# Pooled attention and channel mix: due dates, load order, engines of the first chunks' small steps, and the generator's clock changed

## The chip, the cores and the metric

One Trainium2 (trn2) chip, one NeuronCore of it. The metric is the device time of the whole program in microseconds (us), the median of several executions. The engines are named as in the profile: PE (TensorE), DVE (VectorE), ACT (ScalarE), POOL (GpSimd) and SP, whose queue issues every DMA of this kernel.

## What is computed

```python
def _attn_ref(q, k, v):                      # q, k, v: (8, 8, 576, 64), float32
    k_p = k.reshape(B, H, 72, 8, D).mean(axis=3)      # keys and values pooled by 8
    v_p = v.reshape(B, H, 72, 8, D).mean(axis=3)
    scores = scale * np.matmul(q, k_p.transpose(0, 1, 3, 2))
    scores = scores - np.max(scores, axis=-1, keepdims=True)
    attn = np.exp(scores)
    attn = attn / (np.sum(attn, axis=-1, keepdims=True) + 1e-09)
    return np.matmul(attn, v_p)

def _moe_ref(x, mu_k, mu_r, w_k, w_v, w_r):  # x: (8, 576, 512), the heads side by side
    x_prev = x shifted by one token, zero before the first of a batch
    xk = mu_k * x + (1.0 - mu_k) * x_prev
    xr = mu_r * x + (1.0 - mu_r) * x_prev
    k = np.maximum(xk @ w_k, 0.0)            # 512 -> 1024
    v = k * k @ w_v                          # 1024 -> 512
    r = 1.0 / (1.0 + np.exp(-(xr @ w_r)))    # 512 -> 512
    return r * v
```

The three weight matrices come as 8-byte words and are rebuilt as float32 on the chip.

## The kernel before, in words

**Tiling.** The 4608 tokens are worked off in 13 chunks: 128 tokens, then 256, then eleven of 384 (`CHUNKS`). A chunk consists of tiles of 128 tokens, one load of queries (`qs`) each; the first three tiles are tile 0 (chunk 0) and tiles 1 and 2 (chunk 1). Per batch the keys are summed by eight (`keys`, halves p = 0 and 1 from the loads k0, k1; k2 and k3 are batch 1) into the block diagonal `kbd`, the values (`values`, `last_values`) into `vbd`, `vq_main` and `vq_rest`. For a tile: `scores` (PE), `part` (maximum, exponential, sum, normalizing to `px` and `pm`), `transposed` and `transposed_rest`. For a chunk: `attended` (chunks 0 and 1) or `quarters` (from chunk 2 on), `shifted` and `joined` (the mix with the token before), `x_parts` (chunks from 2 on: the float32 operand split into a high and a low part, the low one a subtraction on POOL into `xkl` and `xrl`), then the three matrix products `hidden` (8 column tiles jt, each over four row tiles ct), `gate` and `mixed`. From chunk 2 on each product is three passes, high by high, low by high, high by low; chunks 0 and 1 use float32 operands instead, each matmul of which stands in the trace as two records.

**Small steps of the start.** `convert` rebuilds a weight block of 512 KB as it lands (one ACT and two DVE instructions, lines 540 to 545), `split` makes its high and low part (ACT line 567; line 570 on DVE or POOL by `LOW_BY`). `SUM_BY` says for a load who sums it by eight: "v" DVE, "g" POOL (three instructions of halving, lines 577 and 619), "t" PE (eight matmuls with the identity, line 588, and ACT copies). `NORM_BY` does so for px and pm of a tile, `COPIES_ON_ACT` for the casts of px, `SQUARED_ON_ACT` for how many of the eight squares of chunks 0 and 1 run on ACT instead of DVE.

**What sets the order.** Every step is a Python generator that yields what it wants next: a need (a value made by another step), a slot of a pool, or an engine with a length. `Order` (lines 127 to 244) holds a clock of its own for each engine. It takes the engine that can start first, and on it the step with the earliest due date among those ready then; the step's instructions are issued there, and that is the program order of the engine. The due date is written in the code for each kind of step, less or more a correction from the table `EARLIER`, by the step's name. So lengths, latencies and landing times in the generators are guesses that set only the order; on the chip each engine runs its own list in order and waits by semaphores.

**Loads.** `loads` issues all DMAs on SP in the order of `LOADS` (k0 r0 k1 q0 c0 ...; c0 is the table of constants `given`, r0 and r1 the packed last values), then the rest by tile. A load of keys or values needs a slot `stage`; only one such slot (`stage0`) is there beside three early ones that are used once each, until chunk 0 is done. So k2 waits for the step that empties `stage0`, and what stands behind it on SP waits too. `turned` sends six small copies within SBUF for each batch, on the same queue.

**Matmuls without a use.** `warm` runs WARMING = 4 float32 matmuls of 256 columns on zeros (line 441). `filling` puts up to FILLERS = 40 matmuls of 128 columns on the identity (line 451) wherever the clock of PE finds nothing else ready; its due date lies behind all others.

Of the kernel before, what the change touches and what calls it, by code (L numbers as in the profile page):

```python
# [28 lines left out]
WP = 512  # L29
# [19 lines left out]
    "k0 r0 k1 q0 c0 q2 r1 q1 v1 wk0 wk1 v0 wk2 q3 wk3 k2 wk4 k3 wk5 wk6 wk7 wr0 q4 q5 wr1 v3 wr2 wr3 "  # L49
    "wv0 wv1 wv2 wv3 wv4 wv5 wv6 wv7 v2 "  # L50
)

SUM_BY = {"k0": "t", "k1": "v", "v0": "t", "v1": "t", "r0": "t", "k2": "g", "k3": "v", "v2": "v", "v3": "v", "r1": "t"}

NORM_BY = {0: 'g', 1: 'v', 2: 'v', 3: 'v', 4: 'g', 6: 'g', 5: 'v'}
WARMING = 4
FILLERS = 40

LOW_BY = {"k": "gvgvvvgv", "r": "gvgv", "v": "gvggvggv"}
# [8 lines left out]
SQUARED_ON_ACT = (5, 0)  # L68
COPIES_ON_ACT = (1, 2, 3, 4)

EARLIER = {
# [14 lines left out]
    "x_parts 3 3 1": 11.2, "warm": 417.9, "constants": 235.0, "complements": 284.6, "loads": 285.1,  # L86
# [27 lines left out]
    "first_values": 614.4, "four_banks": 265.3, "late_rest 1": 198.0, "late_rest 0": 240.1, "turned 0": 787.7,  # L114
    "turned 1": 691.2, "turned 2": -23.6, "turned 3": 9.4,
}
PLAN = ""
SPARE = 0.5
# [12 lines left out]
class Order:  # L131
# [8 lines left out]
    def __init__(self):  # L140
        self.free = dict.fromkeys(self.LATENCY, 0.7)
        self.port = dict.fromkeys(self.LATENCY, 0.0)
        self.landed = 0.0
        self.now = 0.0
        self.made = {}
        self.slots = {}
        self.threads = []
        self.table = "exp"
        self.plan = []
        for step in PLAN.split(", ") if PLAN else ():  # L150
            name, _, times = step.partition(" x")
            self.plan += [name] * int(times or 1)
# [14 lines left out]
    def fetched(self, what, kb):  # L167

        self.landed = max(self.now - 0.6 + 2.5, self.landed) + kb / 395.0 + 0.02
        self.make(what, self.landed)  # L170
# [1211 lines left out]
```

## Time and profile before

| | |
|---|---|
| median of 3 executions | 598.63 us (598.63 to 599.83) |
| profiled execution, its time | 597.71 us |
| profiled execution, its span | 595.8 us |
| around the span | 1.9 us |
| PE busy in the span | 588.2 us (99%) |
| DVE, ACT, POOL busy | 348.5, 294.3, 224.9 us |

The span runs from the first to the last instruction of the profiled execution. That execution lies 0.92 us below the median of the three. A row of the timeline gives the start, the length, the engine, the line of the kernel, the operation, what it writes and reads, how many instructions are merged in it and, in brackets, the idle time ahead of it and what ended it.

### The profile page before, as it was taken

How to read it: one execution, taken by the hardware profiler on the slowest of the kernel's cores; microseconds unless marked ns; L12 is line 12 of the kernel's file. 1: busy time of each engine (PE TensorE's matmuls, PEld its weight loads, DVE VectorE, ACT ScalarE, POOL GpSimd, SP SyncE). 2: the span in 40 equal slices, each digit the busy share in tenths (PEclk: the TensorE clock that was granted, in tenths of full speed). 3: DMA queues.
4: the chain of work that ended last, by engine and by line, in shares of the span. 5: the costliest groups of instructions: out<-in, count | busy, mean ns of one | idle time of the engine just before them, and what ended most of it. 6: DMA issues, size and time to landing. Idle time of an engine off the chain costs nothing.

```text
span 595.8 us, 14121 instructions
## 1 busy us (share of the span) xinstructions
PE 588.2 (99%) x5822; PEld 508.3 (85%) x5822; DVE 348.5 (58%) x709; ACT 294.3 (49%) x574; POOL 224.9 (38%) x350
## 2 busy tenths in 40 slices
PE   9999999999999999999999999999999999999997
PEld 8986458888989989988988988988988988988985
DVE  4989956876438725944814944664824833834411
ACT  4777665844462453553642552462652643554420
POOL 2520269458051552346232257148114115115000
PEclk9999999999999999999999999999999999999999
DMA  8697422442005214113003221521201101000001
GB/s 308 212 390 287 157 77 89 137 157 72 2 19 204 73 46 165 73 57 96 20 12 120 95 73 57 192 73 56 78 2 62 47 1 40 15 3 36 19 0 53
DMA packets 23055, 54.72 MB, mean 92 GB/s; under 512 B 2896, under 2 KB 6352, under 8 KB 22992
## 3 DMA queue, kind: packets, MB, share of 16 engines
q1 hardware_dynamic: 22992, 53.82, 25.8%
q8 instruction: 46, 0.75, 0.5%
q14 instruction: 17, 0.14, 0.1%
HBM read 41.23 MB, written 9.44 MB: 85 GB/s over the span
## 4 chain that ended last, share of the span: by engine, by line
PE 84%; DVE 5%; POOL 4%; DMA 3%; ACT 2%; issue 1%; SPq 1%; DVEq 0%; POOLq 0%; ACTq 0%
PE mm L1264 26%; PE mm L1182 24%; PE mm L1231 11%; PE bank L1182 6%; PE quad L1033 4%; PE bank L1231 4%; PE bank L1264 4%; PE quad L795 3%; DMA got_wr<-in_w_r 2%; POOL stage L577 1%; POOL xkl L1153 1%; POOL xrl L1153 1%; PE own L441 1%; DVE xm L1127 1%; DVE stage L577 1%
## 5 line engine op out<-in xcount | busy, mean ns | idle before, releaser
L1182 PE MATMUL mm<-xkh,w_k 128*128 128x384 f32 x576 | 147.5, 336 | 1.2 <-DVE rk L1199 0.9
L1264 PE MATMUL mm<-w_v,sh 128*128 128x512 f32 x464 | 146.8, 392 | 0.0
L1127 DVE SCALAR_TENSOR_TENSOR xm<-quad,given,t 128x384 f32<-128x384 f32 x88 | 50.3, 613 | 109.2 <-ACT t L1085 72.5
L1182 PEld LDWEIGHTS mm<-xkh,w_k 128*128 128x128 f32 x576 | 103.6, 188 | 3.2 <-DVE rk L1199 1.7
L1264 PEld LDWEIGHTS mm<-w_v,sh 128*128 128x128 f32 x464 | 87.1, 188 | 19.0
L1182 PE MATMUL mm<-xkl,w_k 128*128 128x384 f32 x288 | 96.5, 335 | 0.5 <-POOL xkl L1153 0.5
L1264 PE MATMUL mm<-w_v,sl 128*128 128x512 f32 x232 | 90.4, 390 | 0.0
L1205 ACT CAST sh<-rk 128x384 fp32r<-128x384 f32 x88 | 45.1, 512 | 58.8 <-DVE rk L1199 58.6
L881 POOL TENSOR_TENSOR px<-e,sm 128x64 f32<-128x64 f32 (+1 forms) x33 | 13.7, 414 | 157.3 <-DVE sm L871 79.9
L1231 PE MATMUL mm<-w_r,xrh 128*128 128x512 f32 x192 | 61.3, 391 | 0.0
L1207 DVE TENSOR_TENSOR sl<-rk,sh 128x384 fp32r<-128x384 f32 x88 | 53.4, 608 | 12.8 <-ACT sh L1205 12.7
L1274 DVE TENSOR_TENSOR rs<-mm,rs 128x512 f32<-128x512 f32 x32 | 22.0, 688 | 64.9 <-PE mm L1264 64.5
L1153 POOL TENSOR_TENSOR xkl<-xm,xkh 128x384 fp32r<-128x384 f32 x44 | 44.3, 1019 | 41.3 <-ACT xkh L1151 41.3
L1182 PEld LDWEIGHTS mm<-xkl,w_k 128*128 128x128 f32 x288 | 54.1, 188 | 1.1 <-POOL xkl L1153 1.1
L1192 ACT ACTIVATE rk<-mm 128x384 f32<-128x384 f32 x72 | 35.0, 487 | 39.4 <-PE mm L1182 38.4
L1085 ACT ACTIVATE t<-quad,om_sb 128x384 f32<-128x384 f32 x88 | 44.9, 580 | 17.7 <-PE quad L1033 17.7
L1264 PEld LDWEIGHTS mm<-w_v,sl 128*128 128x128 f32 x232 | 43.6, 188 | 8.8
L577 POOL TENSOR_TENSOR stage<-stage 128x512 f32<-128x512 f32 (+4 forms) x56 | 48.1, 862 | 7.5 <-DMA stage<-in_vm 4.9
L1153 POOL TENSOR_TENSOR xrl<-xm,xrh 128x384 fp32r<-128x384 f32 x44 | 44.3, 1017 | 3.0 <-ACT xrh L1151 3.0
L1199 DVE SCALAR_TENSOR_TENSOR rk<-mm,rk 128x384 f32<-128x384 f32 x72 | 39.6, 550 | 8.3 <-ACT rk L1192 7.2
L1231 PEld LDWEIGHTS mm<-w_r,xrh 128*128 128x128 f32 x192 | 36.0, 188 | 7.7
L1231 PE MATMUL mm<-w_r,xrl 128*128 128x512 f32 x96 | 37.5, 390 | 0.0
(159 smaller groups left out, 978.6 us busy)
## 6 DMA issues: line engine op xcount, KB each, us to landing
qs<-in_qT SPq DMA_DIRECT2D x36, 256.0 KB, 4.1
out<-rs SPq DMA_DIRECT2D x36, 256.0 KB, 2.0
stage<-in_kT SPq DMA_DIRECT2D x15, 576.0 KB, 5.4
stage<-in_vm SPq DMA_DIRECT2D x15, 512.0 KB, 6.2
got_wk<-in_w_k SPq DMA_DIRECT2D x8, 512.0 KB, 6.8
got_wv<-in_w_v SPq DMA_DIRECT2D x8, 512.0 KB, 10.4
stage<-in_vr SPq DMA_DIRECT2D x6, 512.0 KB, 3.5
got_wr<-in_w_r SPq DMA_DIRECT2D x4, 512.0 KB, 8.6
```

The lines of the kernel that those rows point to most:

```text
L577: nc_eng.tensor_tensor(out=st[:, :, :w], in0=st[:, :, :w], in1=st[:, :, w:2 * w], op=ALU.add)
L1033: nc.tensor.matmul(out=out[m * D:(m + 1) * D, t, g], lhsT=w, rhs=p, start=(j == 0), stop=(j == 2),)
L1085: nc.scalar.activation(out=by_token(ts[m][:, 1:n + 1]), in_=xp, func=AF.Copy, scale=om_sb[:, m, g:g + 1])
L1127: nc.vector.scalar_tensor_tensor(out=by_token(xm[:, :n]), in0=bank[:, :n] if c in WHOLE_ATT else bank, scalar=mu_sb[:, m, g:g + 1], in1=by ...
L1153: nc.gpsimd.tensor_tensor(out=lo, in0=xm[:, :n], in1=hi, op=ALU.subtract)
L1182: nc.tensor.matmul(out=hp, lhsT=w[:, o], rhs=x[:, ct, :n], start=(ct == 0 and k == 0), stop=(ct == NCT - 1 and k == len(terms) - 1),)
L1192: nc.scalar.activation(out=rk[:, :n], in_=hp, func=AF.Relu)
L1199: nc.vector.scalar_tensor_tensor(out=rk[:, :n], in0=hp, scalar=0.0, in1=rk[:, :n], op0=ALU.max, op1=ALU.mult)
L1205: nc.scalar.copy(out=sh[:, :n], in_=rk[:, :n])
L1207: nc.vector.tensor_tensor(out=operand("sl", c)[:, jt, :n], in0=rk[:, :n], in1=sh[:, :n], op=ALU.subtract)
L1231: nc.tensor.matmul(out=bank, lhsT=x[:, ct, o], rhs=w, start=(ct == 0 and k == 0), stop=(ct == NCT - 1 and k == len(terms) - 1),)
L1264: nc.tensor.matmul(out=bank, lhsT=s[:, o], rhs=w, start=(jt == 0 and k == 0), stop=(jt == NJT - 1 and k == len(terms) - 1),)
```

## The change

It replaces four kinds of things, and leaves what is computed as it is.

- Tables: the order of the loads, the engines of sums, normalizing, casts, squares and low parts for the first chunks, and the whole table `EARLIER` (new names in it reach into chunk 4).
- The clock of `Order`: an issue on SP counts 0.45 us instead of 0.6, a load lands 2.3 us after its issue instead of 2.5 plus its size, the third load 1.0 us later; at most eight loads are out at a time; work on PE that starts before 6.2 us counts double; two kinds of steps on the four joined banks exclude each other; ACT table loads are no longer charged.
- Lengths of a few steps (the last halving of keys, `quarters`, `warm`, `convert`).
- `filling` may place 70 matmuls instead of 40, but stops once the last x of chunk 0 is made; its own due date moves behind. The fourth `attended` of chunk 0 takes its bank from "bank" instead of "mm".

```diff
 LOADS = (
-    "k0 r0 k1 q0 c0 q2 r1 q1 v1 wk0 wk1 v0 wk2 q3 wk3 k2 wk4 k3 wk5 wk6 wk7 wr0 q4 q5 wr1 v3 wr2 wr3 "
-    "wv0 wv1 wv2 wv3 wv4 wv5 wv6 wv7 v2 "
+    "k0 k1 c0 wk0 r1 q0 v1 q1 r0 q2 wk1 v0 wk3 k3 q3 wk2 k2 q4 wk5 wr0 wk4 v2 wr3 wr2 wk7 wk6 wr1 q5 "
+    "wv0 v3 wv3 wv5 wv6 wv1 wv2 wv4 wv7 "
 )
-SUM_BY = {"k0": "t", "k1": "v", "v0": "t", "v1": "t", "r0": "t", "k2": "g", "k3": "v", "v2": "v", "v3": "v", "r1": "t"}
-NORM_BY = {0: 'g', 1: 'v', 2: 'v', 3: 'v', 4: 'g', 6: 'g', 5: 'v'}
+SUM_BY = {"k0": "g", "k1": "t", "v0": "t", "v1": "t", "r0": "g", "k2": "v", "k3": "v", "v2": "v", "v3": "v", "r1": "v"}
+NORM_BY = {0: "g", 1: "v", 2: "g", 3: "g", 4: "g", 6: "v", 5: "g", 8: "v", 7: "g"}
 WARMING = 4
-FILLERS = 40
-LOW_BY = {"k": "gvgvvvgv", "r": "gvgv", "v": "gvggvggv"}
+FILLERS = 70
+LOW_BY = {"k": "vggggvgg", "r": "ggvv", "v": "vvvvvggv"}
-SQUARED_ON_ACT = (5, 0)
-COPIES_ON_ACT = (1, 2, 3, 4)
+SQUARED_ON_ACT = (7, 6)
+COPIES_ON_ACT = (3, 4)
 EARLIER = {
-    "filling": 764.8, "last_values 1": 76.4, "convert k 0": 615.4, "split k 0": 105.8, "convert k 1": 655.3,
+    "gathered 0": 142.1, "gathered 1": 356.0, "gathered 2": 412.6, "gathered 3": -24.1, "gathered 4": 43.0,
...
+ISSUE = 0.45
+HICCUP = 1.0
+QUEUES = 8
+IN_MM = 4
+COLD = 6.2
...
     def fetched(self, what, kb):
-        self.landed = max(self.now - 0.6 + 2.5, self.landed) + kb / 395.0 + 0.02
+        late = HICCUP if len(self.lands) == 2 else 0.0
+        self.landed = max(self.now - ISSUE + 2.3, self.landed + late) + kb / 400.0 + 0.01
+        self.lands.append(self.landed)
         self.make(what, self.landed)
...
+                if eng == "sp" and len(self.lands) >= QUEUES:
+                    at = max(at, self.lands[-QUEUES])
+                if t[2][3:] and t[2][3] == "quad" and self.joint[0] != eng:
+                    at = max(at, self.joint[1])
...
-            func = t[2][3] if len(t[2]) > 3 else None
-            if func and func != self.table:
-                length, self.table = length + 1.3, func
+            if eng == "pe" and at < COLD:
+                length *= 2
...
         for _ in range(WARMING):
-            yield "pe", 0.43, False
+            yield "pe", 0.86, False
             nc.tensor.matmul(out=bank[:, :256], lhsT=zeros[:, :P], rhs=zeros[:, :256], start=True, stop=True)
...
         for _ in range(FILLERS):
+            if ("x", 0, NPAIR - 1, 0) in order.made:
+                break
             yield "pe", 0.222, False
...
-        bank = yield take("mm" if c in WHOLE and g == NPAIR - 1 else "bank")
+        bank = yield take("mm" if c in WHOLE and g >= IN_MM else "bank")
...
-    order.add(60, filling())
+    order.add(5000, filling())
```

**PE at the start.** The first instructions of PE up to the scores of the first tile (`kbd` by `qs`). `own` with `tmp` is the warm matmul, `bank` with `ident` the filler, `mm` with `ident` the sum of a load of keys, `mm` with `given` that of a packed load. Line numbers of the changed kernel are 26 to 28 higher. Before:

```order
L441 MATMUL own_122<-tmp_102 128x256 x4
L451 MATMUL bank_114<-ident 128x128 x7
L588 MATMUL mm_115<-stage_107,ident 128x144 x8
L451 MATMUL bank_114<-ident 128x128 x3
L669 MATMUL mm_116<-packed,given 128x128 x2
L803 MATMUL sc_121<-kbd_68,qs_104 128x144 x4
```

Now:

```order
L467 MATMUL own_122<-tmp_102 128x256 x3
L616 MATMUL mm_115<-early_sl,ident 128x144 x8
L467 MATMUL own_122<-tmp_102 128x256
L697 MATMUL mm_116<-early_sl,given 128x128 x2
L831 MATMUL sc_121<-kbd_68,qs_104 128x144 x4
L479 MATMUL bank_114<-ident 128x128 x2
L831 MATMUL mm_115<-kbd_68,qs_105 128x144 x2
L831 MATMUL mm_116<-kbd_68,qs_105 128x144 x2
L697 MATMUL mm_117<-packed,given 128x128 x2
```

The sum on PE is now that of k1 (in `early_sl`), not of k0; it stands behind three warm matmuls with no filler between, and ten fillers ahead of the first scores are gone. Over the whole program PE has 22 fillers where it had 40.

**PE where chunk 2 begins.** The end of `mixed` of chunk 1 (`sh`) and of chunk 0 (`stage_109`), and the first `hidden` of chunk 2 (128x384; `xkl` is the low part that POOL makes). Before:

```order
L1264 MATMUL mm_117<-got_wv_530,stage_109 128x512
L1264 MATMUL mm_117<-got_wv_538,stage_109 128x512
L1182 MATMUL mm_116<-xkh_914,w_k_552 128x384 x2
L1182 MATMUL mm_116<-xkl_915,w_k_552 128x384
L1182 MATMUL mm_116<-xkh_914,w_k_552 128x384 x2
L1182 MATMUL mm_116<-xkl_915,w_k_552 128x384
```

Now:

```order
L1292 MATMUL mm_115<-got_wv_570,stage_109 128x512
L1292 MATMUL mm_115<-got_wv_576,stage_109 128x512
L1210 MATMUL mm_117<-xkh_896,w_k_494 128x384 x2
L1210 MATMUL mm_117<-xkl_897,w_k_494 128x384
L1210 MATMUL mm_116<-xkh_896,w_k_573 128x384 x2
L1210 MATMUL mm_116<-xkl_897,w_k_573 128x384
L1210 MATMUL mm_116<-xkh_896,w_k_573 128x384 x2
L1210 MATMUL mm_116<-xkl_897,w_k_573 128x384
L1210 MATMUL mm_117<-xkh_896,w_k_494 128x384 x2
L1210 MATMUL mm_117<-xkl_897,w_k_494 128x384
L1292 MATMUL mm_115<-got_wv_553,stage_109 128x512
```

`hidden` of chunk 2 now begins with five `mixed` matmuls of chunk 0 still to come, two column tiles of it side by side, one row tile at a time.

**ACT where chunk 3 begins.** The copies of values into `vq_main`, the exponential of a tile (`e`) and the first `Relu` of chunk 3 (`rk` from `mm`). Before:

```order
L1151 CAST xrh_1469<-xm_84 128x384
L1151 CAST xrh_1469<-xm_82 128x384
L647 COPY vq_main_72<-stage_108 128x128
L647 COPY vq_main_72<-stage_107 128x128
L866 ACTIVATE e_88<-e_88 128x576
L1192 ACTIVATE rk_85<-mm_117 128x384
```

Now:

```order
L675 COPY vq_main_72<-stage_107 128x128
L1179 CAST xkh_1437<-xm_84 128x384
L1113 ACTIVATE t_81<-quad,om_sb 128x384 x2
L1179 CAST xrh_1446<-xm_82 128x384
L1113 ACTIVATE t_80<-quad,om_sb 128x384 x2
L1179 CAST xkh_1437<-xm_84 128x384
L1179 CAST xkh_1437<-xm_82 128x384
L1179 CAST xrh_1446<-xm_84 128x384
L1179 CAST xrh_1446<-xm_82 128x384
L675 COPY vq_main_72<-stage_108 128x128
L894 ACTIVATE e_88<-e_88 128x576
L1220 ACTIVATE rk_86<-mm_115 128x384
```

One of the two copies has moved ahead, in among the casts of chunk 3.

## Rows read from the trace of the kernel before

**Rows 1.** The page: engines, busy us, share of the span, instructions.
```profile
PE 588.2 (99%) x5822; PEld 508.3 (85%) x5822; DVE 348.5 (58%) x709; ACT 294.3 (49%) x574; POOL 224.9 (38%) x350
```
**Rows 2.** Waits of PE, whole span: engine, tile, line, releaser; us, times, longest.
```profile
PE mm L1182 <- DVE rk L1199: 0.9, 1, 0.9
PE mm L1182 <- POOL xkl L1153: 0.5, 1, 0.5
PE own L1071 <- DVE xrh L1127: 0.3, 1, 0.3
```
**Rows 3.** Groups of PE, 0 to 100 us: count | busy us, mean ns.
```profile
L451 PE MATMUL bank<-ident 128*128 128x128 f32 x80 | 11.3, 279 | 0.0
```
**Rows 4.** Timeline of PE, 0 to 33 us.
```profile
1.45 3.78 PE L441 MATMUL own<-tmp 128*128 128x256 f32 x8 [1.45 <-DVE tmp L437]
5.03 1.95 PE L451 MATMUL bank<-ident 128*128 128x128 f32 x14
6.82 2.13 PE L588 MATMUL mm<-stage,ident 128*128 128x144 f32 x16
8.78 0.83 PE L451 MATMUL bank<-ident 128*128 128x128 f32 x6
...
9.89 1.15 PE L803 MATMUL sc<-kbd,qs 128*128 128x144 f32 x8
...
32.47 0.70 PE L1071 MATMUL own<-pth,vbd 128*128 128x256 f32 x2 [0.30 <-DVE xrh L1127]
```
**Rows 5.** Windows: us, busy of each engine (count), granted clock, DMA share, GB/s.
```profile
1.45:5.49 4.04, 4.04 (x11) 3.33 (x12) 1.02 (x2) 1.28 (x1) 0.42 (x2) 1.00 0.87 281
5.00:10.00 5.00, 5.00 (x42) 4.97 (x41) 1.90 (x5) 0.55 (x2) 0.00 (x0) 1.00 0.97 337
10.00:15.00 5.00, 4.98 (x43) 4.79 (x42) 4.11 (x13) 4.40 (x18) 2.74 (x6) 1.00 1.01 397
50.00:70.00 20.00, 19.94 (x122) 10.45 (x121) 19.70 (x47) 15.43 (x26) 3.34 (x4) 1.00 0.48 171
```
**Rows 6.** DMA issues, 0 to 12 us: count, KB each, median us from issue to landing.
```profile
stage<-in_kT SPq DMA_DIRECT2D x1, 576.0 KB, 3.9
```
**Rows 7.** Timeline: issue of k0, DVE's wait for k1, a sum of keys on POOL.
```profile
0.74 0.38 SPq L523 DMA_DIRECT2D stage<-in_kT  x1
7.48 0.76 DVE L577 TENSOR_TENSOR early_sl<-early_sl 128x576 f32<-128x576 f32 x1 [4.94 <-DMA early_sl<-in_kT]
22.49 1.40 POOL L577 TENSOR_TENSOR stage<-stage 128x576 f32<-128x576 f32 x1 [0.40 <-DMA stage<-in_kT]
25.44 1.46 POOL L619 TENSOR_TENSOR kbd<-stage 64x144 f32<-64x144 f32 x2
```
**Rows 8.** Timeline of PE, 77 to 93 us; last, a piece of the chain that ended last.
```profile
77.67 0.70 PE L1264 MATMUL mm<-got_wv,sh 128*128 128x512 f32 x1
88.53 0.91 PE L1182 MATMUL mm<-xkh,w_k 128*128 128x384 f32 x2
92.44 0.51 PE L1182 MATMUL mm<-xkh,w_k 128*128 128x384 f32 x2
185.96 16.67 PE mm L1182 x96
```
**Rows 9.** Timeline, 142 to 147 us: PE, then ACT.
```profile
144.42 0.34 PE L1182 MATMUL mm<-xkl,w_k 128*128 128x384 f32 x1
146.61 0.62 PE L1182 MATMUL mm<-xkh,w_k 128*128 128x384 f32 x2 [0.95 <-DVE rk L1199]
142.68 0.30 ACT L647 COPY vq_main<-stage 128x128 f32<-128x128 f32 x1 [2.30 <-POOL stage L577]
```
**Rows 10.** Last of six value copies on SP, landing of such copies, first of `quarters` 2.
```profile
65.38 0.59 SPq L657 DMA_DIRECT2D vq_main<-vq_main  x1
vq_main<-vq_main SPq DMA_DIRECT2D x2, 32.0 KB, 3.8
75.13 0.59 PE L1033 MATMUL quad<-pth,vq_main 32*64 32x96 f32 x32
```

More of the change, by code (lines that the diff above doesn't have):

```diff
@@ L67 @@
 BESIDE = (1,)
-SQUARED_ON_ACT = (5, 0)
-COPIES_ON_ACT = (1, 2, 3, 4)
+SQUARED_ON_ACT = (7, 6)
+COPIES_ON_ACT = (3, 4)
 EARLIER = {
[14 rows of a table removed]
-    "x_parts 3 3 1": 11.2, "warm": 417.9, "constants": 235.0, "complements": 284.6, "loads": 285.1,
[27 rows of a table removed]
-    "first_values": 614.4, "four_banks": 265.3, "late_rest 1": 198.0, "late_rest 0": 240.1, "turned 0": 787.7,
-    "turned 1": 691.2, "turned 2": -23.6, "turned 3": 9.4,
+    "gathered 0": 142.1, "gathered 1": 356.0, "gathered 2": 412.6, "gathered 3": -24.1, "gathered 4": 43.0,
+    "gathered 5": 457.3, "gathered 6": 33.8, "gathered 7": -74.6, "gathered 8": -170.5, "four_banks": 262.2,
+    "warm": 28.3, "constants": -28.6, "complements": -25.3, "loads": 517.0, "keys 0 0": -54.3, "values 0 0": 45.9,
[49 rows of a table added]
 }
 PLAN = ""
+ISSUE = 0.45
[3 more added lines that the diff above has]
+COLD = 6.2
 SPARE = 0.5
@@ L147, in __init__ @@
         self.threads = []
-        self.table = "exp"
+        self.lands = []
+        self.joint = ("", 0.0)
         self.plan = []
@@ L167, in fetched, with sent @@
     def fetched(self, what, kb):
-        self.landed = max(self.now - 0.6 + 2.5, self.landed) + kb / 395.0 + 0.02
+        late = HICCUP if len(self.lands) == 2 else 0.0
+        self.landed = max(self.now - ISSUE + 2.3, self.landed + late) + kb / 400.0 + 0.01
+        self.lands.append(self.landed)
         self.make(what, self.landed)
+    def sent(self, kb, n=1):
+        self.landed = max(self.now - ISSUE + 2.0, self.landed) + n * kb / 400.0
+        self.lands += [self.landed] * n
+        self.now = self.landed
     @staticmethod
@@ L228, in run @@
             eng, length, lock = t[2][:3]
-            func = t[2][3] if len(t[2]) > 3 else None
-            if func and func != self.table:
-                length, self.table = length + 1.3, func
+            if eng == "pe" and at < COLD:
+                length *= 2
+            if t[2][3:] and t[2][3] == "quad":
+                self.joint = (eng, at + length + self.LATENCY[eng])
             self.free[eng] = at + length
@@ L248, in act @@
 def act(n, func=None):
-    return "act", 0.1 + n / 1200, False, func
+    return "act", (0.15 if func == "convert" else 0.1) + n / 1200, False
 def pool(n):
@@ L482, in load @@
         if kind == "c":
-            yield "sp", 0.6, False
+            yield "sp", ISSUE, False
             nc.sync.dma_start(out=given, in_=consts)
@@ L489, in load @@
             qs = yield take("qs")
-            yield "sp", 0.6, False
+            yield "sp", ISSUE, False
             nc.sync.dma_start(out=qs, in_=qT[i])
@@ L495, in load @@
         if kind[0] == "w":
-            yield "sp", 0.6, False
+            yield "sp", ISSUE, False
             got = sb.tile([P, 2 * WP], I32, name=f"got_{kind}{i}", tag="w", bufs=WBUFS)
@@ L509, in load @@
                 packed[i] = st[:, :4 * D].rearrange("p (k g n) -> p k g n", k=2, g=2)
-            yield "sp", 0.6, False
+            yield "sp", ISSUE, False
             nc.sync.dma_start(out=packed[i], in_=vp[PACKED.index(i)])
@@ L520, in load @@
         st = yield take("stage")
-        yield "sp", 0.6, False
+        yield "sp", ISSUE, False
         v = st[:rows, :2 * POOL * cols].rearrange("p (g n) -> p g n", g=2)
@@ L538, in convert @@
         t = ff.bitcast(I32)
-        yield act(WP)
+        yield act(WP, "convert")
         nc.scalar.activation(out=ff, in_=top.bitcast(F32), func=AF.Prelu, scale=REBASE, alpha=-2.0 ** 32)
@@ L615, in keys @@
                 halve(on, v, KEYS, n)
-            yield ("dve", 0.284, True) if eng == "v" else ("pool", 0.87, True)
+            yield ("dve", 0.57, True) if eng == "v" else ("pool", 1.3, True)
             for h2 in range(2):
@@ L657, in turned @@
             nc.sync.dma_start(out=vq_main[b % 2][:32 * s, s], in_=src[P - 32 * s:])
-        order.now += 2.5
+            order.sent(64, 2)
         order.make(("turned", b))
@@ L848, in part @@
             )
-            yield "act", 1.2 * na, False, "exp"
+            yield "act", 1.2 * na, False
             for a in range(a0, a1):
@@ L1017, in quarters @@
         hi = yield take("hi")
-        yield "pe", 2.75, False
+        yield "pe", 2.6, False, "quad"
         main = operand("pth", c).rearrange("p g n -> p (g n)").rearrange("p (i j k) -> p i j k", j=16, k=32)
@@ L1082, in shifted @@
         ts = [operand(f"x{'kr'[m]}h", c)[:, g] if whole else t[:, m] for m in range(2)]
-        yield "act", 2 * (act(n)[1] + 0.05), False
+        yield "act", 2 * (act(n)[1] + 0.05), False, "quad" if c not in WHOLE_ATT else None
         for m in range(2):
@@ L1124, in joined @@
             ts = t[:, m, :n]
-        yield "dve", 0.134 + n / 960, False
+        yield "dve", 0.134 + n / 960, False, "quad" if c not in WHOLE_ATT else None
         by_token = (lambda t: t) if c in WHOLE_ATT else (lambda t: t.rearrange("p (t n) -> p t n", t=4))
@@ L1140, in joined @@
             else:
-                order.give("mm" if whole and g == NPAIR - 1 else "bank", bank)
+                order.give("mm" if whole and g >= IN_MM else "bank", bank)
         if direct:
@@ L1276, in mixed @@
         at = starts[c] + tt * P
-        yield "sp", 0.6, False
+        yield "sp", ISSUE, False
         nc.sync.dma_start(out=out[at:at + P, :], in_=rs)
-        order.now += 2.5
+        order.sent(256)
         order.give("rs", rs)
```

89 rows, old and new, of the table EARLIER are left out of this document.

## The prediction

> **What bounds the kernel now.** I read the page first: PE is busy 99% of the span, every other engine at most 58% [rows 1]. Then the waits of PE: beside the 1.4 us before its first matmul the trace names only three, 1.7 us in all [rows 2]. So PE sets the time, and whatever PE does or waits for adds to it in full. But "busy" is not work. The groups of PE hold 80 records of the filler, two for each of 40 matmuls that nobody uses [rows 3]; fourteen of them take 1.79 us from 5.03 to the sum of k0, six take 0.67 us after it [rows 4], so one filler is 0.223 us, and 40 are 8.9 us. Third, stretches that are called busy and are too long: I compared starts. Twelve matmuls of the first `hidden` of chunk 2 take 3.91 us from 88.53 to 92.44, where 96 later ones take 16.67, that is 0.174 each [rows 8]; 1.8 us are lost there. Four take 2.19 us from 144.42 to 146.61 [rows 9], 1.5 us lost. The change moves no matmul with a use out of the program. So all it can bring is fillers left out, less waits put in their place, and those two losses of 3.3 us. Last I read the clock's pace at the start, since the column of the granted clock says 1.00 there [rows 5] and does not agree with the steps: eight warm records of 256 columns take 3.58 us, 1.75 ns a column; sixteen records of 144 columns take 1.96 us, 0.85 ns a column [rows 4]. The first is the 1.2 GHz level, the second 2.4. PE went to the higher level among the first fillers, after 4.0 us of work without a gap (about 1.45 to 5.5).
>
> **The start, step by step.** Three warm matmuls are six records of 0.447 us: PE is done at 4.1. The next thing in its order is the sum of k1, with no filler between. When does k1 land? k0 lands at 0.74 + 3.9 = 4.6 [rows 6, 7]. In the kernel before k1 was the third load and landed at 7.45 [rows 7]; now it is the second, 128 KB nearer. At the 397 GB/s of the next windows [rows 5] its 0.59 MB take 1.5 us: 6.1 at the earliest; with all the delay of before but r0's 128 KB, 0.13 MB at 337 to 397 GB/s, some 0.35 us: 7.1 at the latest. PE therefore stands idle for 2.0 to 3.0 us, after only 2.7 us of work. Whether it then runs at 1.2 or 2.4 GHz no row shows, because before there was never such a gap; so the bounds are the whole sum at 2.4, as the sum of k0 ran before, and the whole sum at 1.2, as the warm records did.
>
> At the higher level: the sum takes 1.96 us, the fourth warm matmul and the sum of r1 0.45 each, so the first scores could start at 9.0 to 10.0; they also need q0, which by the bytes ahead of it (0.99 MB after k1, at 337 to 397 GB/s, 2.5 to 2.9 us) lands near 9.8, and k0, which POOL sums in about 4.4 us as the sum of keys from 22.49 to 26.90 [rows 7]: 4.6 + 4.4 = 9.0. So 9.8 to 10.0, against 9.89 before [rows 4]: **+0.0**. At the lower level the sum takes 3.92 us, the two others up to 0.9 each: 11.1 to 12.0, **+1.2 to +2.1**, of which I take +1.5 as the clock may rise before the sum is over. I take the lower level as likelier: the row nearest to it is the warm stretch, at whose end, after 2.7 us, PE was still at 1.2 GHz, and now a gap follows instead of more work. The Trainium skill ("TensorE: Matmul & The Clock Gate", Part 1) says that the low rate is the default, that activity releases it and idling brings it back; by that rule the sum of k1 runs at the low rate, +1.5, and the trace agrees as far as its slow first records go; nothing here shows a fall after a gap.
>
> From the first scores to the third `attended` of chunk 1, which starts at 32.47 [rows 4], before had 28 fillers, now 22: -6 x 0.223 = -1.3. Work before that point is equal (the scores of tile 3, 0.7, stand ahead of it now and three `hidden` matmuls of 0.223 behind). New waits on PE: tile 1's q1 lands at about 12.1 (1.78 MB behind k1), some 0.7 late at the higher level, hidden by the delay at the lower; transposes of tile 2, whose px and pm now come from POOL (0.2 and 1.0 us) behind two carry copies, 0 to 1.0; others about 0.35. An old wait, 0.3 (0.47 by the starts), goes. Sum: -0.7 to +0.7. The waits stand where the fillers stood, because DVE (4.1 of 5 us busy from 10 to 15 [rows 5]) leads the softmax and is not much relieved: it loses the sum of k1 and pm of tile 2, and gets casts and the sum of k3. I take **+0.2**.
>
> **Later terms.** Two fillers near 40 us are gone: **-0.45**. At chunk 2 the last low part is wanted later: before, `mixed` ran 13 float32 matmuls in 10.86 us after the quarters (77.67 to 88.53 [rows 8]), 0.84 each, and the last of four low parts was wanted eleven matmuls on, at 12.8 us, and came about 1.8 later. Now ten float32 matmuls, twenty of 0.174, two more of 0.84 and one set of scores (0.7) lie ahead of the last: 14.3. If POOL is as late as before (14.5) nearly all of the 1.8 goes; a low part in between can still be late, so 0 to -1.8, taken **-1.0**. At chunk 3 the 1.5 us come from ACT: a value copy waited 2.3 us for POOL and stood ahead of the exponential and the first Relu [rows 9], so a bank came free late. One of two such copies moves ahead, the other waits for POOL rows that stand before the last low part: 0 to -1.5, taken **-0.8**. More squares on ACT (13 for 5) and fewer low parts of w_k on DVE (2 for 5) cost nothing on the path and relieve DVE, which is full from 50 to 70 (19.70 of 20 [rows 5]); if that cover went, PE would wait for weights. From there PE has the same matmuls, at 0.174 each.
>
> Sum at the lower level: +1.5 + 0.2 - 0.45 - 1.0 - 0.8 = **-0.55 us**. The profiled execution took 597.71, so 597.2; it lies 0.92 below the median of the runs, hence 598.1 on that scale.
>
> **Rivals.** A: *the clock is up when k1 lands.* For it: PE works before the gap too, and at the time when k1 lands it had long been up before. Against: then it had worked without a gap. Then the term +1.5 is 0: -2.05, 596.6. This is also how the change would do most of what its count of fillers says.
>
> B: *the changed clock does nothing that PE feels*: the waits take up every filler left out and move the low parts' lateness along (0 for chunk 2 and chunk 3), at the lower level: +1.5 + 0.2 - 0.45 = +1.25, 599.9, on the edge of slower. For it: the generator doubles 0.86 us for each early warm matmul, so its PE is busy until after 6 us and never sees the gap; against: rows 8 and 9 are waits whose causes stand elsewhere in the new lists.
>
> C, slower: *the value copies of batch 1 come too late for the quarters of chunk 2.* On PE these quarters have moved ahead of `mixed` of chunk 0: PE reaches them at about 73.4 instead of 75.13 [rows 10]. On ACT the second copy stands behind the sigmoid of chunk 0's gate, near 66; six SP issues (3.7 us) and a landing of 3.8 us end at about 73. Before, the last issue was at 65.38, so they were there by 69.2 [rows 10], six us early. For it: DVE, which sums those values, is full to 70. Against: DVE is relieved. It decides once the copy on ACT comes after 66.5; 2.5 us late, the price is 2.5 on top of the forecast: +1.95, 600.6, since PE does nothing else and the low parts follow.
>
> **How the numbers follow.** 0.2% is 1.2 us, about what a measurement of this kernel can tell from no change: faster is below 597.4, slower above 599.8. Chances: the forecast 0.45, A 0.27, B 0.13, C 0.15. All the forecast's bounds added up reach from -3.25 to +2.35; they will hardly all fall on one side, so I count it from -2.3 to +1.5 and give it 0.13 faster, 0.30 same and 0.02 slower. A is 0.22 faster, 0.05 same. B is 0.06 same, 0.07 slower. C is 0.02 same, 0.13 slower. Together: faster 0.35, same 0.43, slower 0.22. The time is that of the forecast, 598.1. The range goes from 595.8 (A with the loss at chunk 2 gone whole: 0.2 - 0.45 - 1.8 - 0.8 = -2.85) to 600.5 (B with the late end of the first term: 2.1 + 0.2 - 0.45 = +1.85); it leaves out the worse half of C and the best end of A. The forecast's own range is 596.3 to 600.1.
>
> **What would show it.** In the profile after: 44 filler records for 80; PE idle from about 4.1 until k1 lands at 6 to 7; the sixteen records of its sum in 3.9 us (lower level, forecast) or 2.0 (A); the first scores at 11 to 12 (forecast) or near 9.9 (A); the third `attended` of chunk 1 at about 34. The twelve first matmuls of chunk 2 with less than 1 us lost besides the matmuls of `mixed` between them, and no long wait near 140 to 147. C would show as PE waiting for a DMA of `vq_main` at the quarters near 73 us. The prediction is wrong if the first scores come before 9.5, or if PE waits over 1 us for weights between 35 and 70, which I give no term.

## The result and the profile after

The changed kernel takes **607.51 us** in the median of four executions (606.66 to 608.84), the kernel before beside it 598.63: the ratio is 1.0149, with a 95% interval of 1.012 to 1.0178. Ten executions of it were timed in all (605.11 to 610.65, median 607.89). The forecast was 598.1 with a range to 600.5, so it failed by 9 us. The profiled execution took 606.75 with a span of 605.0, against 597.71 and 595.8 before; the 9.2 us between the two spans are what has to be found.

First the page's engines and the waits of PE in the changed kernel (columns as in [rows 1] and [rows 2]).

```profile
PE 586.3 (97%) x5786; PEld 503.8 (83%) x5786; DVE 348.0 (58%) x703; ACT 293.6 (49%) x578; POOL 223.5 (37%) x352
```

```profile
PE quad L1061 <- issue: 3.2, 4, 1.2
PE quad L823 <- DVE xm L1155: 1.8, 1, 1.8
PE mm L1292 <- DVE got_wv L573: 1.7, 1, 1.7
PE mm L616 <- POOL stage L605: 1.6, 1, 1.6
...
PE mm L1259 <- ACT rs L1267: 1.3, 1, 1.3
PE mm L1259 <- DVE rk L1227: 0.8, 1, 0.8
```

PE runs 36 records less than in [rows 1], the fillers, and is busy 1.9 us less, but waits for things that [rows 2] did not have. The dearest has no releaser at all: "issue", four times, inside `quarters`.

To place the loss I took the starts of all matmuls with a use, in both profiles, and compared the times at which equal amounts of matmul work were done. This is worked out from the two traces; up to 100 us, where the two orders differ, it is good to about half a microsecond:

```
before, us    45.7   59.9   77.1   94.0  115.3  158.3  168.4  209.6  260.7  311.8    end
after later   -1.0   +0.1   +4.1   +4.0   +4.6   +4.9   +5.6   +6.9   +7.6   +9.0   +9.2
```

The kernel is ahead at 45 us, loses 5 us by 77, and the rest in small jumps up to 312; nothing after that. Four things make the table.

**The weights of `mixed`, 46 to 73 us.** SP's timeline, then two rows of ACT, then PE's:

```profile
35.16 0.50 SPq L527 DMA_DIRECT2D got_wv<-in_w_v  x1
46.37 0.33 SPq L551 DMA_DIRECT2D stage<-in_vm  x1
46.74 4.39 SPq L527 DMA_DIRECT2D got_wv<-in_w_v  x7
...
45.01 0.68 ACT L568 ACTIVATE tmp<-got_wv 128x512 f32<-128x512 f32 x1
46.04 0.30 ACT L675 COPY vq_main<-stage 128x128 f32<-128x128 f32 x1
...
62.94 3.70 PE L1259 MATMUL mm<-got_wr,stage 128*128 128x512 f32 x8 [1.32 <-ACT rs L1267]
72.61 1.12 PE L1292 MATMUL mm<-got_wv,sh 128*128 128x512 f32 x2 [1.68 <-DVE got_wv L573]
```

The load of v3 stands second to wv0 in the new list and needs the buffer `stage`. ACT empties it with the copy at 46.04, which stands behind the conversion of wv0, so SP issues nothing from 35.66 to 46.37, and seven weight loads queue behind. Of SP's wait 5.1 us end with DVE's sum of v2, the other 5.6 with this copy. From 43 to 48 us the DMA engines were busy for a share of 0.21 only. The last of the seven is issued at 50.33 and lands 10.7 us later. PE then waits twice: ACT's sigmoid stands behind a late conversion, and a matmul needs the last block itself. By the starts the two cost 1.38 and 1.74 us.

**Holes within `quarters`.** A hole is idle time of PE in the midst of the step, where the profile shows nothing that it waits for. PE's timeline in chunk 2, and the hole in chunk 7:

```profile
77.45 0.58 PE L1061 MATMUL quad<-pth,vq_main 32*64 32x96 f32 x25
79.23 0.30 PE L1061 MATMUL quad<-pth,vq_main 32*64 32x96 f32 x2 [1.19 <-issue]
```
```profile
313.35 0.32 PE L1061 MATMUL quad<-pth,vq_main 32*64 32x96 f32 x5 [1.15 <-issue]
```

`quarters` is 192 small matmuls and as many weight loads, 2.37 us without a hole, some 6 ns an instruction. By the starts the holes of chunks 2, 4, 6 and 7 are 1.43, 0.60, 0.72 and 1.39 us; the kernel before has none. The page's DMA part names the queue:

```profile
q8 instruction: 46, 0.75, 0.5%
```

46 packets of 16 KB are 0.75 MB; PE has 11,572 matmuls and weight loads, so this is its instruction stream, some 64 bytes each and some 256 to a packet. The packets' times in the trace, beside the steps (before: the packet comes in the last quarter of a step or outside it):

```
                 step starts   packet, from the step's start   hole ends, after the packet's end
after, chunk 2      76.24        +0.73 for 0.96                    79.23, 1.3 later
after, chunk 4     161.61        -0.50 for 1.39                   164.02, 1.5 later
after, chunk 6     263.33        -0.17 for 1.22                   265.90, 1.5 later
after, chunk 7     309.93        +0.98 for 0.88                   313.35, 1.6 later
before, chunk 2     75.13        +1.92 for 1.45                   none
before, chunk 7    302.33        +2.51 for 0.96                   none
```

**A wait at chunk 3.** It takes the place of the 1.5 us of [rows 9]:

```profile
144.05 0.73 PE L823 MATMUL quad<-kbd,qs 64*64 64x72 f32 x32 [1.83 <-DVE xm L1155]
```

**The start.** PE's timeline, of the changed kernel's profile and of a second one taken later (called *again* below):

```profile
1.45 2.93 PE L467 MATMUL own<-tmp 128*128 128x256 f32 x6 [1.45 <-DVE tmp L463]
6.02 2.20 PE L616 MATMUL mm<-early_sl,ident 128*128 128x144 f32 x16 [1.65 <-POOL stage L605]
...
9.12 1.22 PE L831 MATMUL sc<-kbd,qs 128*128 128x144 f32 x8
```
```profile
6.23 4.18 PE L616 MATMUL mm<-early_sl,ident 128*128 128x144 f32 x16 [1.85 <-POOL stage L605]
...
11.21 1.15 PE L831 MATMUL sc<-kbd,qs 128*128 128x144 f32 x8
```

The same sixteen records take 2.20 us in one execution and 4.18 in the other: the higher and the lower level of PE's clock. The trace puts the rise at 4.40 and at 10.46 us.

### The profile page after: what moved, and what is told of

It is laid out like the page before. It is cut to its first block, busy times and chain, and to the rows that moved or that the text cites. A ratio compares the mean times of both kernels' runs of the same rounds, so it can differ in the third digit from the quotient of the medians.

```text
span 605.0 us, 14037 instructions
## 1 busy us (share of the span) xinstructions
PE 586.3 (97%) x5786; PEld 503.8 (83%) x5786; DVE 348.0 (58%) x703; ACT 293.6 (49%) x578; POOL 223.5 (37%) x352
## 4 chain that ended last, share of the span: by engine, by line
PE 74%; DVE 8%; DMA 5%; POOL 5%; ACT 4%; issue 2%; SPq 2%; POOLq 0%; ACTq 0%; DVEq 0%
PE mm L1292 24%; PE mm L1210 20%; PE mm L1259 10%; PE bank L1210 6%; PE bank L1259 4%; PE quad L1061 4%; PE bank L1292 4%; PE quad L823 2%; DMA got_wv<-in_w_v 1%; DMA got_wk<-in_w_k 1%; DMA qs<-in_qT 1%; POOL xkl L1181 1%; DVE sl L1235 1%; POOL stage L605 1%; POOL xrl L1181 1%
## 5 line engine op out<-in xcount | busy, mean ns | idle before, releaser
L1210 PE MATMUL mm<-xkh,w_k 128*128 128x384 f32 x576 | 148.3, 338 | 0.3 <-DVE rk L1227 0.3
L1210 PEld LDWEIGHTS mm<-xkh,w_k 128*128 128x128 f32 x576 | 103.5, 188 | 2.9 <-issue 1.0
L1210 PE MATMUL mm<-xkl,w_k 128*128 128x384 f32 x288 | 96.5, 335 | 0.6 <-POOL xkl L1181 0.6
L909 POOL TENSOR_TENSOR px<-e,sm 128x64 f32<-128x64 f32 (+1 forms) x34 | 11.7, 345 | 173.6 <-DVE sm L903 169.1
L1210 PEld LDWEIGHTS mm<-xkl,w_k 128*128 128x128 f32 x288 | 54.0, 188 | 1.3 <-POOL xkl L1181 1.2
```

The costliest lines, as they stand in the source:

```text
L1210: nc.tensor.matmul(out=hp, lhsT=w[:, o], rhs=x[:, ct, :n], start=(ct == 0 and k == 0), stop=(ct == NCT - 1 and k == len(terms) - 1),)
```

## The experiments

Each ran beside the kernel before on the same chip, whose medians were 598.88, 598.93, 598.91 and 598.30 us. Where steps move, a written list of the steps (`PLAN`) keeps the rest in order.

**1. Other places in the instruction stream** (*shift_after*).

```diff
         for _ in range(WARMING):
             yield "pe", 0.86, False
             nc.tensor.matmul(out=bank[:, :256], lhsT=zeros[:, :P], rhs=zeros[:, :256], start=True, stop=True)
+        for _ in range(18):
+            nc.tensor.matmul(out=bank[:16, :16], lhsT=zeros[:, :16], rhs=zeros[:, :16], start=True, stop=True)
```

> The changed kernel with 18 tiny matmuls (16 columns) more on TensorE behind the four warm-up matmuls, so that every later TensorE instruction stands 72 places further on in the stream; nothing else moves. In the changed kernel's trace a quarters step has a hole of 1.43, 0.60, 0.72 and 1.39 us in four of eleven chunks, each within 2 us of an instruction fetch of 16 KB for TensorE, and no semaphore stands there. Theory F (the holes are instruction fetches that come too late because of where the 256-instruction blocks fall): with the blocks falling as in the kernel before, no hole over 0.2 us in any quarters step, span 605.0 - 4.1 = 600.9 us (600.2 to 601.6). Rival (the holes are waits for data, a bank or the value copies that the profile does not name): the holes stay where they are, 604.4 to 606. The matmuls themselves lie in the 1.85 us in which TensorE waits for the first key sum.

Measured: 604.95 us, ratio 1.0105 (1.0085 to 1.0124), span 603.0. No hole is left in any of the eleven steps. The span fell by 2.0 and not 4.1, because in this execution the clock rose only at 12.12 us: at 45 us of the kernel before, this one was 3.1 us behind the changed kernel's profile, at the end 2.0 ahead. Of the 5.1 us gained in between the holes are 4.1 by their lengths; by the starts it gained 0.7, 0.8 and 1.3 us where the holes of chunks 4, 6 and 7 had stood. The first of the two waits for the weights, 1.3 us, is also missing from its waits, since PE came there later; some of that is lost again in short waits of chunk 2. Instructions that do nothing removed the holes.

**2. v3 behind the weights** (*v3_last*).

```diff
-    "wv0 v3 wv3 wv5 wv6 wv1 wv2 wv4 wv7 "
+    "wv0 wv3 wv5 wv6 wv1 wv2 wv4 wv7 v3 "
```

> The changed kernel with the load of v3 moved behind wv7 in the list of loads, and every other instruction in its order. In the changed kernel v3 waits for a stage buffer until 46.37 us and holds up seven weight loads behind it; wv7 lands at 61.01. Theory L (the late weights make the two waits of TensorE of 1.38 us at 61.0 and 1.74 us at 70.3): the weights are issued some 8 to 11 us earlier, wv7 lands by 56, both waits go, span 605.0 - 3.1 = 601.9 us (601.2 to 602.8). Rival 1 (the order of the conversions on ScalarE and VectorE holds those two places, not the landing): under 0.7 us gained, 604.3 or more. Rival 2 (v3, now last, comes too late for its sum at 67.7 on VectorE, and the value copies and the quarters of chunk 2 go later): a new wait ahead of the quarters, 603 to 606.

Measured: 605.70 us, ratio 1.0116 (1.0096 to 1.0136), span 603.5. SP's timeline, and PE's waits from 40 to 80 us:

```profile
35.29 9.16 SPq L527 DMA_DIRECT2D got_wv<-in_w_v  x8
47.06 0.33 SPq L551 DMA_DIRECT2D stage<-in_vm  x1
```
```profile
PE quad L1061 <- issue: 1.1, 1, 1.1
PE mm L1210 <- DVE sh L1227: 0.6, 1, 0.6
PE mm L1210 <- ACT stage L1220: 0.5, 1, 0.5
PE mm L1292 <- DVE got_wv L573: 0.2, 1, 0.2
```

The last weights are issued before 44.5 and land 10.2 us on, near 54.3; v3 lands in time; of the 3.1 us of waits 0.2 is left. From 45 to 77 us it gained the 3.1 us expected on the changed kernel. Theory L holds. The span gained only 1.5: at 45 us it was 0.7 behind the changed kernel's profile, and the holes were 1.32, 0.80, 1.57 and 1.39 us this time, 0.9 more in all. They vary from one execution to the next.

**3. The scores of tile 11 later** (*scores_later*): a list of steps puts them behind the first four steps of `hidden` of chunk 3.

```diff
-softmax 11
 turned 3
...
 last_values 3
-softmax 11
 hidden 3 0
...
 last_values 3
-softmax 11
 hidden 3 0
 last_values 3
+hidden 3 0
 softmax 11
-hidden 3 0
+softmax 11
+softmax 11
+softmax 11
```

> The changed kernel with the scores of tile 11 (32 matmuls) moved on TensorE from ahead of the first hidden block of chunk 3 to behind its twelve matmuls, by a list of steps; the order of all else is kept but for four small VectorE and ScalarE steps of that tile. In the changed kernel these scores wait 1.8 us at 141.8 for VectorE to read the last product out of the joint banks. Theory S (the wait is lost time of its own): 605.0 - 1.7 = 603.3 us (602.7 to 604.0), no wait over 0.5 us between 138 and 148. Rival (the hidden block needs the same steps of VectorE and GpSimd, the wait only moves to its first matmul): 604.4 to 605.5.

Measured: 611.79 us, ratio 1.0217 (1.0198 to 1.0236), span 609.8: 4 us slower than the changed kernel. PE's waits from 140 to 154 us, and a window of L1210 alone, in which 0.55 is the granted clock:

```profile
PE mm L1210 <- POOL xkl L1181: 2.7, 1, 2.7
```
```profile
147.00:150.00 3.00, 2.37 (x7) 1.86 (x7) 0.55 0.40 133
```

The rival was right that the wait only moves (to POOL's last low part), and missed that it costs twice: after it the clock is at the lower level, by the trace from 147.33 to 150.74 us, so 3.4 us do the work of 1.7.

**4. The kernel before, shifted** (*shift_before*).

```diff
-        for _ in range(FILLERS):
+        for n in range(FILLERS):
             yield "pe", 0.222, False
+            if n >= 14 and n % 3 != 1:
+                continue
             nc.tensor.matmul(out=bank[:, :P], lhsT=ident, rhs=ident, start=True, stop=True)
```

> The kernel before with 18 of its 40 fillers left out (they only keep TensorE busy in waits), so that its TensorE stream stands 72 places earlier from 27 us on; nothing else moves. By theory F, with the places of the changed kernel's quarters as the yardstick: holes of about 1.4, 0.6, 1.4, 0.7 and 1.4 us in the quarters steps at 75, 157, 203, 257 and 302 us of the kernel before, where it has none, span 595.8 + 5.5 = 601.3 us (600 to 602.5). Rival (waits for data): no holes, 595.2 to 596.4; or the clock falls where the fillers are missing, which the granted clock between 18 and 30 us would show.

Measured: 605.64 us, ratio 1.0117 (1.0098 to 1.0136). The profiled execution was the slowest of the five, 607.47 with a span of 605.6. It has holes of 0.24, 3.41, 0.64 and 1.34 us in chunks 4 to 7, none in chunk 2. The row at the second, and windows behind it:

```profile
209.56 0.45 PE L1035 MATMUL quad<-pth,vq_main 32*64 32x96 f32 x6 [3.17 <-issue]
```
```profile
206.00:208.80 2.80, 0.39 (x32) 0.22 (x20) 0.87 (x2) 2.00 (x3) 2.64 (x4) 1.00 0.18 67
208.80:215.60 6.80, 6.04 (x39) 4.75 (x39) 0.00 (x0) 0.00 (x0) 3.48 (x6) 0.50 0.01 4
```

Taking 18 useless matmuls out of the kernel before, and nothing else, makes it 6.8 us slower. Four of the five places were forecast right; the sizes vary, and the longest hole takes the clock along: 3.4 us of hole and 6.8 us at half rate. So the kernel before is fast partly because its blocks fall well.

The traces settle this more firmly than the times do. I counted the records of TensorE's two queues ahead of the first matmul behind each hole: over all thirteen profiles there are 17 holes of 0.2 us or more. They stand 249 to 337 instructions into the step, yet the count leaves 193 in each when it is divided by 256: the place in the step varies, the place in the stream does not, and a wait for data or a bank would have it the other way round. With this place taken as the start of a block, `quarters` of chunks 2 to 7 begin:

```
places into a block     steps   with a hole
175 to 221                 16        15
7 to 12                     5         2
30 to 84, 247 to 255       57         0
```

The steps of the first two rows are of the changed order without added matmuls (*after*, as the changed kernel's profile is called here, *again*, *v3_last* and *scores_later*) and of *shift_before*; all 36 steps of the six profiles with 18 matmuls added stand in the last row, whenever their clock rose.

**5. Both repairs** (*both*): v3 last as in 2, and the tiny matmuls behind the third warm-up matmul.

```diff
+            for _ in range(18 if n == 2 else 0):
+                nc.tensor.matmul(out=bank[:16, :16], lhsT=zeros[:, :16], rhs=zeros[:, :16], start=True, stop=True)
```

> The changed kernel with both repairs: v3 loaded behind wv7, and 18 tiny matmuls on TensorE (here directly behind the third warm-up matmul, in the wait for the first key sum), so that the instruction blocks fall as in the kernel before. If the late weights (2.7 us in the run with v3 last) and the instruction fetches (4.1 us) add up: 605.0 - 6.8 = 598.2 us where TensorE's clock rises within the first 6 us, up to 3 us more where it rises at 12. Rival (the two share time, since the hole at 77.8 us follows the late weights): 599.5 or more with an early clock.

Measured: 602.70 us, ratio 1.0075 (1.0048 to 1.0101), span 601.6. At 115 us of the kernel before it is 2.6 us behind it (the changed kernel 4.6), at 312 us 5.7 (9.0). The sum of k1 took 4.18 us again. New is that the clock fell from 143.60 to 147.02 us, behind the wait at chunk 3; every one of the six executions had a mean clock of 0.995 to 0.997. With the later rise (+1.7 at 60 us against the changed kernel's profile) and the fall (+1.6 by the same comparison of starts) the two repairs add up: 605.0 - 6.8 + 1.7 + 1.6 = 601.5.

**6. Work in the idle stretch of the start** (*both_warm*), on experiment 5.

```diff
+            for _ in range(4 if n == 2 else 1):
                 nc.tensor.matmul(out=bank[:, :256], lhsT=zeros[:, :P], rhs=zeros[:, :256], start=True, stop=True)
-            for _ in range(18 if n == 2 else 0):
+            for _ in range(15 if n == 2 else 0):
```

> As the run with both repairs, but of the 18 added matmuls three are full warm-up matmuls of 256 columns, 2 us of work, in the stretch from 4.2 to 6.0 us in which TensorE stood idle; 15 are tiny. The clock rose at 4.4, 5.1, 10.8 and 12.1 us in four executions of this start. Theory C (the idle stretch is what leaves the clock low in some executions): the clock rises by 6.5 us, every run shows a mean granted clock of 0.999 or 1.000, spans lie within 1.5 us of each other, median 1 us below the run with both repairs. Rival (chance of the execution alone): the spread of 2 to 3 us stays.

Measured: 602.25 us, ratio 1.0066 (1.0044 to 1.0089), spans 600.0 to 601.7 (599.7 to 602.9 in experiment 5). The clock rose at 6.53 us, the sum of k1 took 2.23, but began at 7.58 behind the added work; the first scores came at 10.52. The mean clock, 0.996 to 0.998, missed its forecast, since it fell at chunk 3 here too; of the start it says nothing, for it is 1.000 in the profile of *shift_after*, whose clock rose at 12.12. Experiments 8 and 9 have the same start, and their clock rose at 6.98 and 6.64 us. So theory C is supported by three profiles of three, against two early rises in the seven of the changed order without the three full matmuls. The spread of the spans says nothing: it is 0.8 us in experiment 7 without them and 3.6 in experiment 8 with them.

**7. GpSimd's sums first** (*both_pool*), on experiment 5: three steps of POOL.

```diff
 quarters 3
+values 3 0
+values 3 0
+values 3 0
 softmax 9
...
-values 3 0
...
-values 3 0
...
-values 3 0
```

> As the run with both repairs, and the three sums of the values 3 0 on GpSimd stand ahead of tile 9's and 10's products there: GpSimd stands idle from 110 to 130 us in its order and does those sums (2.6 us) at 137.7 and 143.3, among the parts of chunk 3. Theory P (GpSimd's queue makes the wait of 1.8 us for the last product of chunk 3 in the joint banks): that wait falls to 0.4 us or less, 1.3 us below the run with both repairs at the same clock, 596.9 us. Rival (ScalarE and VectorE read the joint banks in turn and are just as late): under 0.4 us gained.

Measured: 603.23 us, ratio 1.008 (1.0057 to 1.0103). A miss: PE's waits from 120 to 145 us show the old wait whole and a new one ahead of the quarters.

```profile
PE quad L825 <- DVE xm L1157: 1.9, 1, 1.9
PE quad L1063 <- DVE pth L956: 1.5, 1, 1.5
```

The new one comes from DVE, which makes `pth` 1.5 us later than in *both*. While POOL does the three sums, two instructions of DVE take 2.21 us for 0.61, here POOL and DVE, then DVE in *both*:

```profile
119.14 3.00 POOL L607 TENSOR_TENSOR stage<-stage 128x512 f32<-128x512 f32 x3 [10.81 <-DMA stage<-in_vm]
119.57 2.21 DVE L649 TENSOR_TENSOR kbd<-stage 64x144 f32<-64x144 f32 x2
```
```profile
119.83 0.61 DVE L649 TENSOR_TENSOR kbd<-stage 64x144 f32<-64x144 f32 x2
```

**8. The sums last** (*sums_after*), on experiment 6, and **9. the scores later as well** (*sums_and_scores*), by the edit of experiment 3.

```diff
-values 3 0
...
-values 3 0
...
-values 3 0
...
 x_parts 3 1 0
+values 3 0
+values 3 0
+values 3 0
```

> As the run with both repairs and three more warm-up matmuls, and GpSimd does the three sums of the values 3 0 behind the last but two of chunk 3's parts instead of among them; all other engines keep their order. In that run TensorE waits 1.9 us at 140 us for the last product in the joint banks, and its clock falls to half from 143.1 to 146.5 us. Theory P2 (these sums lie on the chain of GpSimd and VectorE that frees the joint banks): the wait falls by about 1.2 us, to 0.7, the clock stays up there, 601.3 - 1.2 - 1.7 = 598.4 us. Rival 1 (the chain is bound by ScalarE and VectorE): wait still over 1.5 us, 600.8 or more. Rival 2 (the clock falls for another reason than this wait): 600 us.

> The run with GpSimd's sums moved, and tile 11's scores moved behind the first twelve hidden matmuls of chunk 3 as in the run with the scores later. There the move lost time, since the last low part of chunk 3 came from GpSimd only at 145.5 us, behind the sums; with the sums moved that part is done at 141.4, and TensorE's wait of 1.7 us at 139.4 can be filled with the three matmuls of each part as it comes. Theory Q (the two moves help only together): no wait over 0.7 us between 138 and 146, no fall of the clock there, 599.4 - 1.3 = 598.1 us of span, and a median 2 to 3 us below the run with the sums alone, in most of whose executions the mean clock shows the fall. Rival (the hidden units of chunk 3 then wait for VectorE, which takes the late scores first): 599.4 or more.

Measured: 602.88 us (1.0072, 1.0052 to 1.0091) and 601.96 us (1.0064, 1.0042 to 1.0085). With the sums last the wait is still 1.7 us, as rival 1 said: DVE waits for POOL's low parts one after the other. With the scores moved too, PE waits 1.1 us for POOL and 0.8 for DVE; its profile gained nothing there (rival), but the clock holds: a mean of 0.999 or 1.000 in all six executions, against 0.994 to 0.996 in four of six with the sums alone. Median spans: 601.1 and 600.2.

**10. The kernel before with a late copy** (*before_copy*): ACT's copy that [rows 9] shows, moved behind the exponentials and two hidden steps.

```diff
-values 3 1
 softmax 11
...
 hidden 3 1
...
 hidden 3 1
+values 3 1
```

> The kernel before with one ScalarE step, the copy of the values 3 1 (0.3 us), moved behind the exponentials of tile 11 and two steps of the first hidden block of chunk 3, and the three pairs of turning copies that follow it on SyncE moved likewise; TensorE's order is unchanged. In the kernel before this copy waits 2.3 us for GpSimd at 142.7 us and what stands behind it on ScalarE lets TensorE wait 1.1 us at 145.3. Theory: that wait goes, 595.8 - 1.0 = 594.8 us, the quarters of chunk 4 at 156 us find the turned values there (they land by 152). Rival (GpSimd's sums or the copies of the next step hold the hidden units likewise): 595.4 to 596.4.

Measured: 598.34 us against 598.93, ratio 0.9999 (0.9981 to 1.0018): no difference. The wait at 146.6 is gone, and another of 0.7 us stands ten microseconds later; by the starts the profile gains 0.6 us from 115 to 158, less than the medians can tell:

```profile
155.55 0.62 PE L1182 MATMUL mm<-xkh,w_k 128*128 128x384 f32 x2 [0.70 <-DVE rk L1199]
```

**11. The changed kernel again** (*after_again*).

> The changed kernel as it is, beside the run above on the same chip: 605 to 608 us of span by the level of the clock in the first 12 us, and the four holes in the quarters steps at the places of its first profile (0.5 to 1.6 us each), since these depend on the order of the instructions alone.

Measured: 608.27 us, ratio 1.0152 (1.0121 to 1.0184), spans 603.3 to 608.9. The profile (span 607.2) has one hole of 1.66 us and one of 0.23 instead of four, the late clock at the start shown above, and the fall at chunk 3:

```profile
145.48 0.73 PE L823 MATMUL quad<-kbd,qs 64*64 64x72 f32 x32 [1.83 <-DVE xm L1155]
```
```profile
147.00:150.40 3.40, 3.40 (x12) 3.39 (x11) 1.71 (x4) 1.18 (x2) 3.17 (x5) 0.50 0.41 133
```

The expectation that the holes depend on the order alone was wrong: the order sets where they can stand, the execution decides how long they are and whether they come. No version that beats the kernel before was found.

## Why the prediction was wrong

By its own steps:

- **The start, +1.5.** In the profile it was -0.8: the clock was up for the sum of k1 and the first scores came at 9.12, which is rival A, and which the prediction named as a sign against itself. In three of the five profiles with this idle stretch (*again*, *shift_after*, *scores_later*) the clock rose at 10.46 us or later and the first scores came at 11.2 or later. So both levels happen; the step treated a spread as a choice. It is a spread of some 2 to 3 us, and not what the 9 us hang on.
- **To the third `attended` of chunk 1, +0.2, and two fillers, -0.45.** Right to within a microsecond: 1.0 ahead at 45 us.
- **No term for weights between 35 and 70.** This is the first step that failed. The prediction took the list of loads as a matter of bytes landed and looked for late data in the first 12 us only; that SP holds back what stands behind a load waiting for a buffer is said ahead of it, but v3 was not followed to the buffer it needs, nor to ACT's copy of v2 behind the conversion of wv0. It named a wait of over 1 us for weights there as a sign against itself, and the longer of the two is 1.7. Price: 3.1 us, shown by experiment 2; where the clock rose late, less, as the first of the two waits is then 0.7 us (*again*, *scores_later*) or absent (*shift_after*).
- **"From there PE has the same matmuls, at 0.174 each".** This is the second, larger failure. The matmuls are the same, their places in the stream are not: 4.1 us of holes in the profile, about 3 in the medians (experiment 1), and the reverse in experiment 4. The fillers were priced at 0.223 us each and nothing more, though each is also four instructions that shift all that follow. [rows 1] shows a PE busy for 99% and hides how near to its fetches it runs. The kernel said so itself: both versions hold the call `nc.tensor.addr_align` in `hidden`, which with BLOCK = 256, INTO_BLOCK = 45 and ALIGNED_FROM = 7 sets the place of `quarters` in a block for chunks 8 to 12, and leaves chunks 2 to 7, where all the holes stand, to what comes ahead of them. The Trainium skill ("Runtime: NRT & Kernel Launch", on instruction fetch mechanics) says that instructions come in blocks of 16 KB, 256 of them, and that crossing a block is mostly hidden. The trace agrees on the blocks; the holes of 0.2 to 3.4 us are what is not hidden.
- **Chunk 2, -1.0.** It did not come. The waits are spread over five places between 88 and 108 us, and 0.5 us more is lost than before.
- **Chunk 3, -0.8.** The 1.5 us of [rows 9] went, and the scores' wait of 1.83 us came in their place, which the prediction called a sign against it. It is dearer than it looks, as the clock falls behind it in some executions (1.6 us more; not in the profile of 605.0).
- **Not named at all:** a wait of 0.8 us ahead of a `gate` at 209 us, 1.2 by the table.
- **Rival C**, the slower side, was the wrong mechanism: the value copies were late (the last issued at 72.8 us), but `quarters` of chunk 2 began at 76.25 directly behind the matmul before it.

Sum for the two profiles: -1.0 at 45 us, then 3.1 of weights, 0.7 for a short wait at 50 us, 4.1 of holes, 0.5 at chunk 2, 0.3 at chunk 3, 1.2 at the gate: 8.9 of 9.2. For the medians the last 3.7 us that experiment 9 leaves are the start, chunks 2 and 3 and the gate; how they share them was not tried one by one.

## What to carry to other kernels

In an in-order queue, follow each load to the buffer that it waits for, and price all that stands behind it. Where a step issues instructions every few nanoseconds, look at when the instruction stream's own packets come, and ask of every inserted or removed instruction what it shifts. Setting the place of such steps, as this kernel does from chunk 8 on, was not tried here for chunks 2 to 7. A wait of 2 us on TensorE costs more than itself if the clock falls behind it; work from elsewhere in the order can fill it.

## What was not expected of the hardware

- TensorE goes on 1.3 to 1.6 us after the end of its instruction packet; in a burst of 384 instructions in 2.4 us that is enough for holes of 0.2 to 1.7 us, once 3.4. All 17 holes stop at one place modulo 256 of TensorE's stream. From chunk 8 on, no hole stands in any of the thirteen profiles; there the kernel sets the place of `quarters`, in the trace by a branch at 337.38 us and then 39 empty instructions in each of four chunks.
- The same start gave a rise of the clock at 4.40, 5.10, 10.46, 10.8 and 12.12 us. What decides was not found; with work in the idle stretch it rose at 6.53, 6.64 and 6.98.
- At chunk 3 a wait of 1.7 to 1.9 us was followed by 3.4 us at the lower level in the profiles of *both*, *both_warm* and *again*, and by none in those of *after*, *shift_after*, *v3_last*, *both_pool* and *sums_after*. The wait alone does not settle it.
